# A fixed written issue order on TensorE and GpSimd, loads in pieces, and attention spread over the FFN halves

## The chip, the cores and the metric

The kernel runs on one core of one Trainium2 chip. The metric is the device time of that core in microseconds; a run's time is about 2 us longer than the span (first to last instruction) that its profile shows. Where a ratio stands, it is the mean time of one kernel's fast runs over that of the kernel before in the same rounds on the same chip, so it isn't quite the ratio of the medians that are quoted.

The engines are TensorE (PE in the profile, PEld its weight loads), VectorE (DVE), ScalarE (ACT), GpSimd (POOL) and SyncE (SP). "Issue" in the profile is time in which an engine waited for nothing that the profile shows.

## The reference

Four batches, eight heads, 768 positions, head size 64. Each head's sequence is cut into 8 blocks of 96. A small matrix P (8x8 for each batch and head) is normalized five times over rows and columns (Sinkhorn); it mixes the blocks of k and v; each block of q attends to its mixed block. The result goes through a gated feed-forward network (FFN).

```python
P = sort_net                                        # (4, 8, 8, 8)
for _ in range(5):
    P = np.exp(P - P.max(-1)); P = P / P.sum(-1); P = P / P.sum(-2)   # keepdims left out
k_sorted = einsum('bhij,bhjcd->bhicd', P, k_blocks)
v_sorted = einsum('bhij,bhjcd->bhicd', P, v_blocks)
x = softmax(q_blocks @ k_sorted.T / 8) @ v_sorted   # (3072, 512) after the reshape
g = x @ w_gate                                      # (512, 1536)
out = (silu(g) * (x @ w_val)) @ w_out               # (1536, 512)
```

## The kernel before

A tiling framework orders the instructions of each engine by priority and dependency; the program's text gives the priorities. TensorE does the block mixing with block-diagonal matrices made from P: the products `tkq` mix and transpose k and q together (q with an identity), `tv` mix v. For each unit (4 blocks of 2 heads) there are the scores `qk`, an exp on ScalarE, the attention-value product `av_ps`, on VectorE a reciprocal and the normalization `st`, and the transposition `x_ps` to the FFN's layout. One FFN half is 384 positions: 12 pairs of a gate product `g_ps` and a value product `v_ps` (4 matmuls each), and 3 output groups `o_ps` of 12 matmuls. There are 8 halves and 32 units.

```python
load_kq(0, [0, 24, 48, 72, 96]); make_identity(nc, ident)      # loads on GpSimd's queue
...
load_v(0, 2)
for it in range(5):                                             # Sinkhorn
    nc.scalar.activation(p_sb, p_sb, AF.Exp)
    nc.vector.reduce_sum(rowred[:, :, 0], p_sb, axis=AX.X); nc.vector.reciprocal(rowred, rowred)
    nc.vector.tensor_mul(p_sb, p_sb, rowred.to_broadcast([BH, NB, NB]))
    ...                                                         # the same for columns
# w_ps: P brought onto the partitions of k and v; rmix, vmix: the mixing matrices
...                                                             # weights, then batch 1 to 3
def emit_vch(pair):                                             # v's columns put side by side
    for s in range(4):
        eng = nc.gpsimd if pair else nc.vector
        eng.tensor_copy(vch[:, :, cs], nat[:, cs, :].transpose([0, 2, 1]))
...
emit_att(0)
for b in range(B):
    if b + 1 < B:
        emit_att(b + 1)
    emit_gv(b, 0); emit_gv(b, 1)
    emit_out(b, 0); emit_out(b, 1)
```

The softmax here doesn't subtract the row's maximum and nothing guards it: scores larger than these inputs give would overflow.

## Time and profile before

The median is 286.03 us (285.81 to 286.82). The profile below is of one execution of 287.63 us, with a mean granted clock of 0.968.

| stage (kernel before) | time, us | read from |
|---|---|---|
| normalization ends | 11.9 | timeline of VectorE |
| product w_ps starts | 13.6 | waits of TensorE |
| first score product / first attention-value product | 24.1 / 33.7 | timeline of TensorE |
| first gate product | 36.1 | timeline of TensorE |
| half clock | 35.6 to 49.3, 59.5 to 62.9 | clock records |
| last instruction | 285.9 | page |

The busy times and four rows of the page of the kernel before (each digit is the busy share of one fortieth of the span in tenths; PEclk is the granted TensorE clock):

```profile
PE 257.2 (90%) x2600; PEld 152.7 (53%) x2608; DVE 178.9 (63%) x383; ACT 121.7 (43%) x246; POOL 39.1 (14%) x51
PE   0077799969999999999999999999999999999993
PEclk9999955979999999999999999999999999999999
DMA  6999999999100122000000122000000220000021
```

TensorE is nearly always busy after the first tenth of the span. What there is to win lies at the start and in the two dips of the clock. The largest waits of TensorE before (in all, count, longest):

```profile
PE w_ps L148 <- DVE lmix L142: 13.6, 1, 13.6
PE tkq L193 <- issue: 2.5, 1, 2.5
```

The timeline of TensorE before (start, length, what, count, and in brackets the idle time ahead of it; the view ends at 61 us):

```profile
56.39 0.97 PE L193 MATMUL tkq<-rmix,kq 128*64 128x64 bf16 x45
59.90 1.33 PE L193 MATMUL tkq<-rmix,kq 128*64 128x64 bf16 x42 [2.54 <-issue]
```

### The profile page before, as it was taken

How to read it: one execution, taken by the hardware profiler on the slowest of the kernel's cores; microseconds unless marked ns; L12 is line 12 of the kernel's file. 1: busy time of each engine (PE TensorE's matmuls, PEld its weight loads, DVE VectorE, ACT ScalarE, POOL GpSimd, SP SyncE). 2: the span in 40 equal slices, each digit the busy share in tenths (PEclk: the TensorE clock that was granted, in tenths of full speed). 3: DMA queues.
4: the chain of work that ended last, by engine and by line, in shares of the span. 5: the costliest groups of instructions: out<-in, count | busy, mean ns of one | idle time of the engine just before them, and what ended most of it. 6: DMA issues, size and time to landing. Idle time of an engine off the chain costs nothing.

```text
span 285.9 us, 6221 instructions
## 1 busy us (share of the span) xinstructions
PE 257.2 (90%) x2600; PEld 152.7 (53%) x2608; DVE 178.9 (63%) x383; ACT 121.7 (43%) x246; POOL 39.1 (14%) x51
## 2 busy tenths in 40 slices
PE   0077799969999999999999999999999999999993
PEld 0066555746655446666655446666555445555441
DVE  6798746937988205789988304699885018888300
ACT  2036745437633215976534215764332134343211
POOL 8557421029500000000000000000000000000000
PEclk9999955979999999999999999999999999999999
DMA  6999999999100122000000122000000220000021
GB/s 99 198 203 197 200 213 204 220 214 214 38 0 1 39 110 76 2 2 0 3 0 2 38 110 76 2 2 2 0 0 2 111 102 10 0 0 3 37 110 73
DMA packets 13659, 20.84 MB, mean 73 GB/s; under 512 B 1088, under 2 KB 8768, under 8 KB 13632
## 3 DMA queue, kind: packets, MB, share of 16 engines
q0 software_dynamic: 10128, 14.16, 28.2%
q1 hardware_dynamic: 3504, 6.30, 5.8%
q8 instruction: 20, 0.33, 0.4%
q14 instruction: 7, 0.06, 0.1%
HBM read 28.32 MB, written 6.29 MB: 121 GB/s over the span
## 4 chain that ended last, share of the span: by engine, by line
PE 82%; DVE 11%; ACT 3%; issue 2%; ACTq 0%
PE v_ps L297 22%; PE g_ps L288 22%; PE o_ps L308 22%; PE av_ps L245 4%; PE qk L230 4%; PE tkq L193 3%; PE x_ps L255 3%; PE tv L214 3%; DVE kqt L180 2%; DVE vch L204 1%; DVE st L251 1%; ACT vt L182 1%; DVE vt L180 1%; ACT th_sb L291 1%; DVE colred L136 0%
## 5 line engine op out<-in xcount | busy, mean ns | idle before, releaser
L288 PE MATMUL g_ps<-xt,wg_sb 128*128 128x384 bf16 x384 | 84.8, 331 | 0.2 <-DVE h L299 0.2
L297 PE MATMUL v_ps<-xt,wv_sb 128*128 128x384 bf16 x384 | 82.1, 331 | 0.0
L291 ACT ACTIVATE th_sb<-g_ps 128x384 bf16<-128x384 f32 x96 | 47.1, 491 | 63.2 <-PE g_ps L288 62.6
L293 DVE SCALAR_TENSOR_TENSOR gs_sb<-th_sb,g_ps 128x384 bf16<-128x384 bf16 x96 | 52.9, 551 | 26.9 <-ACT th_sb L291 20.9
L308 PE MATMUL o_ps<-wo_sb,h 128*128 128x512 bf16 x280 | 62.4, 379 | 0.4
L299 DVE SCALAR_TENSOR_TENSOR h<-v_ps,gs_sb 128x384 bf16<-128x384 f32 x96 | 53.1, 553 | 9.0 <-PE v_ps L297 0.8
L297 PEld LDWEIGHTS <-wv_sb 128*128 128x128 bf16 x384 | 36.8, 98 | 24.5 <-issue 0.8
L288 PEld LDWEIGHTS <-wg_sb 128*128 128x128 bf16 x384 | 36.2, 99 | 23.5 <-issue 2.3
L308 PEld LDWEIGHTS <-h 128*128 128x128 bf16 x288 | 28.2, 98 | 33.6
L180 DVE CAST kqt<-tkq 128x512 bf16<-128x512 f32 x24 | 15.9, 688 | 33.9 <-PE tkq L193 33.9
L311 ACT COPY o_sb<-o_ps 128x512 f32<-128x512 f32 x24 | 14.1, 586 | 51.4 <-PE o_ps L308 51.4
L235 ACT ACTIVATE er<-qk 96x384 bf16<-96x384 f32 x64 | 27.1, 487 | 12.2 <-PE qk L230 12.2
L193 PE MATMUL tkq<-rmix,kq 128*64 128x64 bf16 x768 | 20.3, 212 | 5.5 <-issue 2.5
L193 PEld LDWEIGHTS <-kq 128*64 128x64 bf16 x768 | 17.7, 126 | 8.9 <-issue 7.9
L251 DVE TENSOR_TENSOR st<-av_ps,r_sb 96x512 bf16<-96x512 f32 x32 | 21.9, 684 | 0.8
L182 ACT CAST kqt<-tkq 128x512 bf16<-128x512 f32 x24 | 14.1, 586 | 15.7 <-PE tkq L193 15.6
L230 PE MATMUL qk<-kqt 64*128 64x96 bf16 x256 | 14.0, 217 | 1.9 <-DVE kqt L180 1.4
L245 PE MATMUL av_ps<-vt,er 96*128 96x65 bf16 x256 | 14.9, 202 | 0.2 <-ACT vt L182 0.2
L180 DVE CAST vt<-tv 96x512 bf16<-96x512 f32 x16 | 12.2, 785 | 2.7 <-PE tv L214 2.5
L182 ACT CAST vt<-tv 96x512 bf16<-96x512 f32 x16 | 12.5, 787 | 2.1 <-PE tv L214 1.8
L214 PE MATMUL tv<-vmix,vch 128*128 128x128 bf16 x128 | 12.4, 236 | 1.0 <-DVE vt L180 0.3
L255 PEld LDWEIGHTS <-st 96*128 96x128 bf16 x128 | 7.6, 101 | 10.5 <-DVE st L251 9.1
(43 smaller groups left out, 123.0 us busy)
## 6 DMA issues: line engine op xcount, KB each, us to landing
out_dram<-o_sb SPq DMA_DIRECT2D x24, 256.0 KB, 2.0
v<-in_v_dram POOLq DMA_DIRECT2D x8, 384.0 KB, 13.1
kq<-in_k_dram POOLq DMA_DIRECT2D x6, 384.0 KB, 11.6
kq<-in_q_dram POOLq DMA_DIRECT2D x6, 384.0 KB, 12.1
wg_sb<-in_moe_w_gate_dram POOLq DMA_DIRECT2D x6, 256.0 KB, 11.8
wv_sb<-in_moe_w_val_dram POOLq DMA_DIRECT2D x6, 256.0 KB, 11.1
wo_sb<-in_moe_w_out_dram POOLq DMA_DIRECT2D x1, 1536.0 KB, 18.9
kq<-in_k_dram POOLq DMA_DIRECT2D x4, 192.0 KB, 5.6
```

The costliest lines, as they stand in the source:

```text
L180: nc.vector.tensor_copy(dst, src)
L182: nc.scalar.copy(dst, src)
L193: nc.tensor.matmul(tp[two * D:(two + 1) * D, lc, :], lhsT=nat[:, cb * 8 + lc, :], rhs=rm[:, two, :], start=True, stop=True)
L230: nc.tensor.matmul(pss[two][:, i4, :], lhsT=flat[lo:lo + D, at:at + 128], rhs=kqt[lo:lo + D, 1, g, i, :], start=True, stop=True)
L235: nc.scalar.activation(e[:, 0:4 * C], pss[two][0:C].rearrange("p a c -> p (a c)"), AF.Exp, scale=scale)
L245: nc.tensor.matmul(av[:, two, i4, :], lhsT=es[two][:, i4 * C:i4 * C + 128], rhs=vt[:, 2 * g + two, half * 4 + i4, :], start=True, stop=True)
L288: nc.tensor.matmul(g_ps, lhsT=wg_sb[:, kc, ts(m, 128)], rhs=xt[:, kc, :], start=(kc == 0), stop=(kc == NKC - 1))
L291: nc.scalar.activation(th_sb, g_ps, AF.Tanh, scale=0.5)
L293: nc.vector.scalar_tensor_tensor(gs_sb, th_sb, 1.0, g_ps, op0=ALU.add, op1=ALU.mult)
L297: nc.tensor.matmul(v_ps, lhsT=wv_sb[:, kc, ts(m, 128)], rhs=xt[:, kc, :], start=(kc == 0), stop=(kc == NKC - 1))
L299: nc.vector.scalar_tensor_tensor(h_w[:, m, :], v_ps, 0.5, gs_sb, op0=ALU.mult, op1=ALU.mult)
L308: nc.tensor.matmul(o_ps, lhsT=h_w[:, m, ts(t3, 128)], rhs=wo_sb[:, m, :], start=(m == 0), stop=(m == NFC - 1))
```

## The change

The intent: TensorE and GpSimd issue in the order of the program text. Batch 0 and the weights are loaded in pieces, q is mixed while the normalization still runs, only batch 0's half of v is mixed at first, FFN half 0 starts after four units, and the attention of the next batch is spread between the products of the FFN halves. The core of the diff:

```diff
-    load_kq(0, [0, 24, 48, 72, 96])
+    man = tc.manual_schedule(engines={mybir.EngineType.PE, mybir.EngineType.Pool})
+    man.__enter__()
+    load_v(0, 0, HC)
     make_identity(nc, ident)
+    load_v(0, HC, C)
+    load_q(0, 0, HC); load_q(0, HC, C)
+    load_k(0, 0, HC); load_k(0, HC, C)
+    copy_v(nc.gpsimd, 0, lowr, 0)
+    load_gv(0, 256)
+    copy_v(nc.gpsimd, 0, lowr, 1)
+    load_gv(256, 512)
+    copy_v(nc.gpsimd, 0, lowr, 2)
+    copy_v(nc.scalar, 0, lowr, 3)
+    load_gv(512, 768)
     ...                                   # batch 1's k and q, the other weights, v of batch 1
+    for cb in range(6):
+        half_chunk(0, 1, cb, "s", tags[cb % 2])           # q of batch 0, before w_ps
     ...                                   # w_ps, rmix, vmix as before, through a copy w_sb
+    for cb in range(6):
+        half_chunk(0, 0, cb, "vs"[cb % 2], tags[cb % 2])  # k of batch 0
+    ...                                   # qk(0, 0..3) between 8 v_chunk; then av and xtr of 4 units
+    def merge(main, side):                # side items placed in proportion to main's time
     ...
-    emit_att(0)
-    for b in range(B):
-        if b + 1 < B:
-            emit_att(b + 1)
-        emit_gv(b, 0); emit_gv(b, 1); emit_out(b, 0); emit_out(b, 1)
+    merge(ffn(0), units(0, range(4, 8)))
+    nc_b1 = attention(1)
+    merge(ffn(1), nc_b1)
+    for b in range(1, B):
+        first, second = split(attention(b + 1)) if b + 1 < B else ([], [])
+        merge(ffn(2 * b), first)          # ffn(n): 12 pairs of n, 3 output groups of n - 1
+        merge(ffn(2 * b + 1), second)
+    for t3 in range(3):
+        outp(2 * B - 1, t3)
```

A half chunk mixes k or q alone, with 32 matmuls of half the height, where a whole chunk mixes both: 384 matmuls in place of 192 for batch 0.

## The prediction

> **What bounds the kernel now.** TensorE: 257 of 286 us busy on the page, without gaps from 63 to 281 us in the timeline. By start-to-start times four gate or value matmuls cost 0.65 us and twelve output matmuls 2.6 us, so one FFN half is 15.7 + 7.8 = 23.5 us and eight are 188 us at full clock. Where attention units are packed between FFN pairs (126 to 140 us) their period is 2.17 us, VectorE's own work in it (0.55 + 0.55 + 0.20 + 0.68 + half of 0.35). The waste lies before 63 us: TensorE starts at 13.6 us, the first FFN matmul comes at 36.1 us, the clock records show 0.5 from 35.6 to 49.3 us and from 59.5 to 63.0 us, and there are 2.5 us of idle at 57.4 us, where batch 1's last k/q piece had not landed (the queue runs at 200 GB/s until 71 us). [...] the records change in multiples of 3.41 us, and at 28.8 us the tv matmuls go from 107 to 55 ns.
>
> **What the change does, from the issue order on each engine.**
> 1. Batch 0's V evictions (0.79 us each) before the first AV are halved, exps overlap them, and q is mixed during Sinkhorn. But v, q and k land in that order (2.36 MB, about 16.7 us at the rate of before), and four AV units run bare: AV, reciprocal 0.20, transpose copy 0.35, normalise 0.68, about 1.7 us each. I estimate the first FFN matmul at 36 us (34 to 38): no earlier than now.
> 2. From there FFN half 0 is dense, not 3 FFN matmuls per 2.5 us at half clock. Full clock returns after about 5 us: 4 us gained.
> 3. Batch 1's k/q is queued before the later weights (there at about 31 us, needed near 55 us): the 2.5 us idle and its 1.7 us of half clock go.
> 4. Units are spread over two FFN halves for batches 2 and 3: at most 0.2 us gained on each of 20 units, 3 to 4 us.
> 5. Costs: batch 1's V mixing is a second pass, 64 more matmuls, about 2.3 us. Batch 1's attention is pressed into one FFN half: four qk in a row wait for exps on ScalarE (about 2 us), and its last three units run bare after the last output group (about 3 us, perhaps 1.7 us of half clock near 85 to 90 us). Batches 2 and 3 end with one bare unit, 1 us each.
>
> **Sum.** 36 + 188 (FFN) + 39 (attention left) + 2.5 (cold clock) + 10 (stalls) + 4.5 (last copy and store) = about 280 us.
>
> Predicted 280.5 us, range 272 to 289. Faster by over 2%: 0.48; within 2%: 0.46; slower: 0.06.
>
> **What the profile would show.** First gate matmul at 34 to 38 us; half clock for 3 to 7 us from there, then 1.0; no wait for batch 1's k/q; a stretch of low TensorE share near 85 to 90 us with transposes waiting for the normalise step; the last three output groups unchanged.
>
> **What would make it wrong.** A faster start (half-height k/q chunks under 0.6 us would bring the FFN to 33 us); clock drops of several windows after the bare units; Pool's transposing copies (2.9 us each) in its in-order queue holding up loads; ScalarE, which takes all k/q and v evictions, delaying the tanh and so the gate matmuls.

The terms come to 280.0 us. But the 5 us after which full clock was to return, and with them the 4 us gained and the 2.5 us of cold clock, are the author's estimate. In the trace before, half clock lasted 13.7 us from 35.6 us and 3.4 us from 59.5 us; what the change made of it stands under the result.

## The result

The changed kernel takes 303.48 us (303.03 to 303.96, four runs), against 286.09 us (285.81 to 286.82) for the kernel before in the same rounds: ratio 1.0604 (95% interval 1.0577 to 1.0630). It is slower by 6%. The same rows of the page, after:

```profile
PE 260.3 (86%) x2864; PEld 154.5 (51%) x2864; DVE 163.4 (54%) x357; ACT 132.3 (44%) x263; POOL 52.1 (17%) x51
PE   0057667999998959999999989999999999999994
PEclk9999999999999996999999999999999999999998
DMA  6999999198084000100100000000000001000011
```

TensorE is busy for a smaller share of the span than before (86% against 90%), above all in slices 3 to 7. The clock row needs care: ahead of the first clock record, at 54.1 us, it shows full clock, but in this run four gate matmuls take 1.28 us up to 54.1 us and 0.65 us later, so TensorE was at half clock until then. Behind the first gate product there are 12.5 us of half clock in all (48.4 to 54.1 and 112.2 to 119.0 us), against 16.6 us before (36.1 to 49.3 and 59.5 to 62.9), a window behind the last product left out in both, so the clock isn't where the time went. In two parts:

| | before | predicted | after |
|---|---|---|---|
| first gate product, us | 36.1 | 36 | 48.4 |
| from there to the end of the span, us | 249.8 | 244.5 | 253.7 |

The predicted 280.5 us is a run's time, about 2 us longer than a span, so the second row missed by 9 us as it stands and by about 11 in like terms.

**The start, 12.3 us late.** The largest waits of TensorE after:

```profile
PE tkq L200 <- DVE rmix L163: 18.7, 1, 18.7
PE av_ps L279 <- DVE st L285: 5.7, 6, 1.0
PE x_ps L296 <- DVE st L285: 3.8, 4, 1.0
PE tkq L200 <- issue: 3.4, 2, 2.3
PE qk L259 <- ACT e_all L266: 1.8, 3, 0.7
```

The first mixing product waits for a VectorE copy into rmix until 18.7 us, though q's first piece landed at 11.5 us. The timeline of VectorE after shows what held that copy up:

```profile
6.64 2.27 DVE L173 TENSOR_TENSOR p_sb<-p_sb,rowred 32x64 f32<-32x64 f32 x1
8.95 0.25 DVE L174 TENSOR_REDUCE colred<-p_sb 32x8 f32<-32x64 f32 x1
9.46 5.16 DVE L176 TENSOR_TENSOR p_sb<-p_sb,colred 32x64 f32<-32x64 f32 x1
15.41 1.93 DVE L173 TENSOR_TENSOR p_sb<-p_sb,rowred 32x64 f32<-32x64 f32 x1
17.89 0.21 DVE L176 TENSOR_TENSOR p_sb<-p_sb,colred 32x64 f32<-32x64 f32 x1
18.51 0.44 DVE L163 COPY rmix<-ident 64x64 bf16<-64x64 bf16 x4
20.46 0.68 DVE L340 TENSOR_TENSOR lmix<-p_sb,selk 32x512 bf16<-32x512 f32 x1
```

The same multiplication takes 0.21 us when it is left alone, and here once 2.27, once 5.16 and once 1.93 us, while reductions and reciprocals between them keep their length. The timeline of GpSimd after, in the same time:

```profile
6.10 2.73 POOL L113 COPY vch<-v 64x1536 bf16<-64x1536 bf16 x1 [1.08 <-DMA v<-in_v_dram]
10.31 2.77 POOL L113 COPY vch<-v 64x1536 bf16<-64x1536 bf16 x1
14.46 2.79 POOL L113 COPY vch<-v 64x1536 bf16<-64x1536 bf16 x1
```

Each long multiplication ends within 0.2 us of the end or the start of one of these new GpSimd copies. The multiplications read p_sb and rowred or colred, both in SBUF (the memory that this program keeps its tiles in, apart from the products of TensorE, which go to PSUM). The reductions at 6.18 and 14.95 us, which read one tile, keep their 0.21 us beside the copies. The multiplication that began at 9.46 us did so while GpSimd by its records only issued loads (8.79 to 10.33 us), and stood through a whole copy (10.31 to 13.08) and two more issues, until 14.62 us. The issues alone don't lengthen a multiplication: those at 17.89, 19.45 and 20.22 us kept 0.21 us beside them. No run shows why the one at 9.46 us stood. The normalization ends at 20.4 us in place of 11.9, and w_ps starts at 24.0 in place of 13.6.

Then k is mixed. The timeline of TensorE after:

```profile
23.98 0.59 PE L346 MATMUL w_ps<-selb,lmix 32*64 32x4 bf16 x16
25.18 0.59 PE L200 MATMUL tkq<-rmix,kq 64*64 64x32 bf16 x15 [0.61 <-DVE rmix L355]
26.88 3.60 PE L200 MATMUL tkq<-rmix,kq 64*64 64x32 bf16 x128 [1.10 <-issue]
32.80 1.51 PE L200 MATMUL tkq<-rmix,kq 64*64 64x32 bf16 x49 [2.33 <-issue]
34.99 0.50 PE L259 MATMUL qk<-kqt 64*128 64x96 bf16 x8 [0.68 <-ACT kqt L182]
```

All of k landed by 17.2 us, and yet there are two stalls that wait for nothing shown. Between them lie exactly 128 matmuls, with their weight loads 256 instructions. The DMA records have 16 KB reads of TensorE's instructions starting at 24.5, 30.5, 36.6 and 42.7 us: one for every 3.6 us of this work, but 6.1 us apart. TensorE stands for 1.10 us ahead of the 128 matmuls and for 2.33 us behind them. That it waits there for these reads is the reading so far; the runs with held loads below test it.

Behind the k mixing come scores and v mixing, for which the prediction gives no size of its own, and the four bare attention-value units (bare: with no FFN product between them). These take 7.5 us up to the first gate product, where four times 1.7 us was estimated; the second, third and fourth each begin with 1.02 to 1.04 us of waiting for VectorE to empty the one result buffer.

**From the first gate product on, 9 us more than predicted.** TensorE's gaps of over 0.15 us behind it come to 9.2 us, against 3.8 before. Three of the waits lie close together at the end of half 1. The timeline of TensorE after, and then the same kernel in windows of 3.40 us (the clock records of both kernels between the first and the last product change in steps of 3.41 us; columns: window, its length, busy us and count of PE, PEld, DVE, ACT, POOL, then the granted clock, DMA share, GB/s):

```profile
109.61 0.43 PE L279 MATMUL av_ps<-vt,e_all 96*128 96x65 bf16 x8 [1.04 <-DVE st L285]
111.26 0.43 PE L279 MATMUL av_ps<-vt,e_all 96*128 96x65 bf16 x8 [1.05 <-DVE st L285]
112.90 0.50 PE L296 MATMUL x_ps<-ident,st 96*128 96x96 bf16 x4 [1.04 <-DVE st L285]
```

```profile
108.80:112.20 3.40, 1.20 (x24) 0.91 (x24) 2.35 (x8) 0.00 (x0) 0.00 (x0) 0.99 0.20 77
112.20:115.60 3.40, 2.70 (x12) 1.35 (x12) 1.36 (x4) 0.49 (x1) 0.00 (x0) 0.50 0.00 0
```

The window with 1.20 us of work in 3.40 was followed by half clock, for two windows (112.2 to 119.0 us). In the kernel before, windows with 1.96 us (from 32.2 us) and 1.26 us (from 56.1 us) were, and in e12_coarse below one with 1.71 us.

Where the time from the first gate product to the end goes, by product, for four kernels (from the start of a group's first matmul to the start of the next group's first, summed; so a wait counts to the group ahead of it; the last two kernels are experiments below; a few before-kernel units had begun ahead of its first gate product and some of its groups mix in the order, so single rows are good to about 1 us):

| product | before | after | e12_coarse | e8_best |
|---|---|---|---|---|
| gate and value | 134.4 | 136.8 | 134.4 | 133.4 |
| output | 67.0 | 67.6 | 67.2 | 69.3 |
| k and q mixing | 16.8 | 12.8 | 12.8 | 13.5 |
| v mixing | 4.8 | 6.6 | 6.6 | 6.3 |
| scores | 9.6 | 10.9 | 9.8 | 7.3 |
| attention-value | 9.0 | 7.5 | 9.0 | 8.0 |
| transposition | 8.2 | 11.5 | 10.1 | 4.8 |
| sum | 249.8 | 253.7 | 249.8 | 242.6 |

### The profile page after: what moved, and what is told of

It is laid out like the page before. It is cut to its first block, busy times and chain, and to the rows that moved or that the text cites. A ratio compares the mean times of both kernels' runs of the same rounds, so it can differ in the third digit from the quotient of the medians.

```text
span 302.1 us, 6710 instructions
## 1 busy us (share of the span) xinstructions
PE 260.3 (86%) x2864; PEld 154.5 (51%) x2864; DVE 163.4 (54%) x357; ACT 132.3 (44%) x263; POOL 52.1 (17%) x51
## 4 chain that ended last, share of the span: by engine, by line
PE 82%; DVE 10%; ACT 4%; issue 2%; DMA 1%; ACTq 0%
PE g_ps L309 22%; PE o_ps L328 21%; PE v_ps L318 21%; PE tkq L213 4%; PE tkq L200 4%; PE av_ps L279 3%; PE qk L259 3%; DVE st L285 2%; DVE p_sb L176 2%; PE x_ps L296 2%; PE tv L234 2%; DVE p_sb L173 2%; ACT o_sb L331 1%; ACT vt L182 1%; DVE xt L180 1%
## 5 line engine op out<-in xcount | busy, mean ns | idle before, releaser
L182 ACT CAST kqt<-tkq 128x512 bf16<-128x512 f32 x45 | 25.0, 589 | 21.3 <-PE tkq L213 12.3
L113 POOL COPY vch<-v 64x1536 bf16<-64x1536 bf16 (+1 forms) x11 | 30.5, 2810 | 18.8 <-DMA v<-in_v_dram 13.2
L266 ACT ACTIVATE e_all<-qk 96x384 bf16<-96x384 f32 x64 | 27.7, 483 | 11.1 <-PE qk L259 11.1
L200 PE MATMUL tkq<-rmix,kq 64*64 64x32 bf16 x384 | 11.0, 211 | 22.8 <-DVE rmix L163 18.7
L200 PEld LDWEIGHTS <-kq 64*64 64x64 bf16 x384 | 10.7, 152 | 22.9 <-DMA kq<-in_q_dram 11.6
L279 PE MATMUL av_ps<-vt,e_all 96*128 96x65 bf16 x256 | 14.3, 200 | 6.5 <-DVE st L285 5.7
L283 DVE RECIPROCAL r_sb<-av_ps 96x8 f32<-96x8 f32 x32 | 6.4, 199 | 24.4 <-PE av_ps L279 24.4
L182 ACT CAST vt<-tv 96x512 bf16<-96x512 f32 x26 | 17.7, 752 | 2.5 <-PE tv L244 1.2
L279 PEld LDWEIGHTS <-e_all 96*128 96x128 bf16 x256 | 11.9, 102 | 11.3 <-DVE st L285 7.4
L213 PEld LDWEIGHTS <-kq 128*64 128x64 bf16 x576 | 11.3, 113 | 9.4 <-issue 9.4
## 6 DMA issues: line engine op xcount, KB each, us to landing
wg_sb<-in_moe_w_gate_dram POOLq DMA_DIRECT2D x6, 256.0 KB, 11.4
```

The source lines that it names most:

```text
L113: eng.tensor_copy(dst, src)
L182: nc.scalar.copy(dst, src)
L200: nc.tensor.matmul(tp[two * D:(two + 1) * D, lc, :], lhsT=nat[rows, cb * 16 + lc, :], rhs=rmix[b][rows, two, a].rearrange("p g i -> p (g i)"),
L266: nc.scalar.activation(e[:, 0:4 * C], pss[two][0:C].rearrange("p a c -> p (a c)"), AF.Exp, scale=scale)
L279: nc.tensor.matmul(o[:, two, i4, :], lhsT=e[:, i4 * C:i4 * C + 128], rhs=vt[:, 2 * g + two, half * 4 + i4, :], start=True, stop=True)
```

## The experiments

Theories that the experiments tell apart:

- A: GpSimd's early copies block VectorE and so the normalization, in the multiplications (A1) and in the rmix copies (A2); the first gate product is late for that.
- R: in phases of very short products, TensorE waits for its own instructions (1.10 and 2.33 us after), because their refills come late while data loads fill the DMA.
- W: with one result buffer, and with units bunched behind each other, the attention units wait for VectorE and ScalarE, and the gaps bring back the half clock (112.2 to 119.0 us after).
- Rivals: the start is held by loads, or by refills of a fixed duration; VectorE's own rate sets the units' period; spreading costs as much at each switch as it saves.

### Sums kept in PSUM (e1_psum)

```diff
-    rowred = const.tile([BH, NB, 1], FP32)
-    colred = const.tile([BH, 1, NB], FP32)
+    red_ps = psum.tile([BH, 2, NB], FP32, name="red_ps", tag="av", bufs=1)
+    rowred = red_ps[:, 0, :].unsqueeze(2)
+    colred = red_ps[:, 1, :].unsqueeze(1)
```

> The changed kernel with the two Sinkhorn scale vectors in PSUM, so that VectorE's Sinkhorn multiplications read only one operand from SBUF; Pool's copies and loads stay. Theory A [...]: the multiplications take 0.2 to 0.3 us again where they took 1.9 to 5.2, the last Sinkhorn step ends near 12.5 us and not 20.4, the first gate matmul comes at about 41 us and not 48.4, total about 296 us (295 to 298). Rival B ([...] anything else of Pool that slows VectorE whatever it reads): multiplications stay at 2 us or more, total 303.

Measured 298.94 us (ratio 1.042, interval 1.036 to 1.048), just outside the 295 to 298 expected. The timeline of VectorE in this run:

```profile
6.78 0.21 DVE L174 TENSOR_TENSOR p_sb<-p_sb,red_ps 32x64 f32<-32x64 f32 x1
8.91 8.45 DVE L163 COPY rmix<-ident 64x64 bf16<-64x64 bf16 x4
17.39 0.21 DVE L174 TENSOR_TENSOR p_sb<-p_sb,red_ps 32x64 f32<-32x64 f32 x1
```

Every multiplication takes 0.21 us now: the second SBUF operand was what blocked them (A1). But the four rmix copies that now come up in GpSimd's time take 8.45 us in place of 0.44, and the multiplication behind them waits in order. The repair of one instruction moved the block to the next. w_ps starts at 20.9 us and the first gate product at 43.7 us; 4.5 us of the 7.5 us expected came.

### One identity copy on GpSimd (e2_ident), and both repairs (e3_both)

```diff
+    nc.gpsimd.tensor_copy(rmix0[R:2 * R, :, 1, :, :], idq)   # ahead of GpSimd's first v copy
     copy_v(nc.gpsimd, 0, lowr, 0)
     ...
-    for b in range(B):                                       # VectorE's copies: batch 0's is gone
+    for b in range(1, B):
```

> The changed kernel with batch 0's identity block of the mixing matrix written by Pool before its first copy, not by VectorE behind the fourth Sinkhorn iteration; Sinkhorn is left as slow as it is. Theory A: q mixing starts at about 11.6 us (when q has landed) but the weights matmul still waits for Sinkhorn at about 21.2 us, so only the 2.8 us between 21.2 and 24.0 are gained: about 300.5 us. Rival C (what costs the start is the identity copy's place in VectorE's order, not the blocked multiplications): the start moves by about 7 us and the total is about 296.

> Both edits together. Theory A: as with the PSUM edit alone within 1 us (about 296), because with Sinkhorn fast the identity copies come at about 10 us and are no longer late; the start is then bound by the landing of q and k and by two waits of TensorE for instruction blocks (1.1 and 2.3 us in the changed kernel). Rival C: another 3 us or more below the PSUM edit alone.

Measured 298.99 us for the first (ratio 1.0438), between theory A's 300.5 and rival C's 296. q's mixing starts at 11.4 us, the multiplications are blocked as before (2.04, 5.16 and 1.93 us), w_ps starts at 21.0, where A had it, and the first gate product comes at 43.6 us: 3.0 us come from the earlier w_ps, and most of the rest from the k mixing, where one stall of 1.9 us is left of the two (3.4 us).

Measured 295.62 us for both (ratio 1.0317, interval 1.027 to 1.037). That is 3.3 us below the PSUM edit alone, which is what rival C expected of the pair, so by the totals the place of the identity copy in VectorE's order counts too. The profile can't show how: its execution, with a span of 297.0 us, was 3 us longer than the timed ones (293.0 to 294.0). In it the three rmix copies left on VectorE take 8.26 us and the first gate product stays at 43.7 us. As long as the early GpSimd copies are there, these profiles show one VectorE instruction or the other blocked.

### No early copies on GpSimd (e5_nopool)

```diff
-    copy_v(nc.gpsimd, 0, lowr, 0)          # and 1, 2; and 3 on ScalarE
     ...
+    for s in range(4):                     # after rmix and vmix; the first line only makes it wait
+        nc.vector.tensor_copy(vch3[lowr, 0, 24 * s:24 * s + 1], w_sb[0:R, 0, s:s + 1])
+        copy_v(nc.vector, 0, lowr, s)
```

> Only batch 0's four early transposing copies move from GpSimd and ScalarE to VectorE, made to wait for the mixing matrices. Theory A (GpSimd's early copies block VectorE, whatever VectorE does with two SBUF operands or as an SBUF copy): the normalization ends near 12 us instead of 20.4, the weights product w_ps starts near 13, every VectorE multiplication in it takes 0.2 to 0.3 us and every identity copy under 0.5, the first gate product comes near 40 us instead of 48.4, and the total falls to about 293 (291 to 295). Rival B (the start is held by loads and instruction refills, and the blocking only hides behind them): the first gate product stays at 43 or later, as in the run with both partial repairs, and the total stays at 295.5 or more.

Measured 296.45 us (ratio 1.0363, interval 1.033 to 1.040). The timeline of VectorE, then of TensorE:

```profile
6.54 0.21 DVE L169 TENSOR_TENSOR p_sb<-p_sb,rowred 32x64 f32<-32x64 f32 x1
9.69 0.44 DVE L159 COPY rmix<-ident 64x64 bf16<-64x64 bf16 x4
11.64 0.68 DVE L336 TENSOR_TENSOR lmix<-p_sb,selk 32x512 bf16<-32x512 f32 x1
```

```profile
16.70 0.59 PE L342 MATMUL w_ps<-selb,lmix 32*64 32x4 bf16 x16
25.93 1.51 PE L196 MATMUL tkq<-rmix,kq 64*64 64x32 bf16 x49 [2.88 <-issue]
```

k's evictions (the copies of its products out of PSUM), which alternated between VectorE and ScalarE, went to ScalarE alone in the same edit. No VectorE instruction of the normalization is stretched, and it ends at 11.6 us, 8.8 us earlier: A holds. The first gate product comes at 41.4 us, 7.0 us earlier. Two expectations were missed. w_ps was expected near 13 us and starts at 16.7, although lmix is ready at 12.3: in the written order it stands behind q's 192 matmuls, which the fixed order can't pass. And the total was expected at 291 to 295; at 296.45 it lies where rival B had it (295.5 or more), though the first gate product doesn't. That product came 1.4 us later than expected, and from there to the end the kernel took 253.0 us, hardly less than the changed kernel (253.7), with the same two windows of half clock behind the bare units.

### Loads held while k is mixed (e6_hold, e11_hold, e10_both)

```diff
-    load_gv(256, 512)                      # and all later loads, from GpSimd's early order
     ...
     for cb in range(6):
         half_chunk(0, 0, cb, ...)
+    held = const.tile([1, 1], BF16)        # GpSimd waits here for the last k chunk
+    nc.gpsimd.tensor_copy(held, kqt_tile(0)[0:1, GI * C - 1:GI * C])
+    load_gv(256, 512)                      # and all later loads
```

The first two are the changed kernel with this alone (the second is the first once more, timed); the third has it together with the edit of e5_nopool.

> The changed kernel, with all loads after the first weight pieces held back until k is mixed, so that the data queue is empty during the k mixing. Theory R (the two stalls of 1.1 and 2.3 us in the k mixing are refills of TensorE's instructions [...]): both shrink below 0.4 us, and the k mixing takes about 6 us instead of 9. Rival S (a refill takes that long whatever the data queue does, or the stalls have another cause): stalls of 1 us and more stay in the k mixing. The total isn't to be read from this run, since the weights come late on purpose: it may be 300 to 315.

> The changed kernel with only the loads held, timed this time (the look had one execution, 296.9). If holding the loads is worth the refill stalls and the 3 us of half clock less that the look showed, it is 297 (295.5 to 298.5); if that one execution was a chance, 301 or more.

> The run without early GpSimd copies, and in the same kernel the loads after the first weight pieces held until k is mixed. If blocked VectorE and refills behind loads are two separate losses, the stall of 2.9 us in the k mixing goes too and what the two save at the start adds up: the first gate product comes at about 37 to 38 us (41.4 without the hold), and the total is about 292 (290 to 294). Rival (the two overlap, or held weights come late): the first gate product stays after 40 us, or gate products wait for weights, and the total is 295 or more.

The look took 296.91 us (one execution), the timed run 299.20 us (ratio 1.0443, interval 1.039 to 1.049), slower than the 295.5 to 298.5 expected. The timeline of TensorE in the timed run, then of the third kernel:

```profile
24.73 5.30 PE L189 MATMUL tkq<-rmix,kq 64*64 64x32 bf16 x192 [0.62 <-DVE rmix L344]
30.71 0.50 PE L248 MATMUL qk<-kqt 64*128 64x96 bf16 x8 [0.68 <-ACT kqt L171]
```

```profile
17.92 4.96 PE L185 MATMUL tkq<-rmix,kq 64*64 64x32 bf16 x177 [0.91 <-issue]
```

The 192 matmuls of k run through in 5.30 us without a stall. Nothing on TensorE was changed: R holds, as far as the loads are what makes the refills late. (The hold took GpSimd's issuing of the loads out of this stretch as well as their traffic; no run tells the two apart.) A single read of 16 KB takes no longer beside loads: in the changed kernel the four reads from 24.5 to 42.7 us took 0.94 to 1.09 us each, and its later ones, of which most have no loads beside them, 0.88 to 1.45. With loads those four reads are 6.1 us apart. Without loads they follow 3.5 us apart in the third kernel (15.5, 19.0 and 22.5 us) and 5.1 and 3.9 us apart in the timed run, and keep up with the work. What makes the next read start late isn't seen in the records and stays open. Where some of the first weights still load, 0.91 us of the stall is left.

The first gate product comes at 44.0 us with the hold alone, and at 37.3 us with both edits (total 293.08 us, ratio 1.0230, interval 1.017 to 1.029, as expected): 4.4 us from the hold and 7.0 us from the copies make 11.4, and both together bring 11.1, so they are two separate losses. But the hold isn't the refills alone. In the changed kernel the k mixing shrinks from 9.1 to 5.3 us; in the third it shrinks from 9.5 to 6.5 us, and another 1.5 us come from q, whose first piece lands at 9.7 in place of 11.4 us. That the sums agree so well is partly chance, and in these executions the loads hold the start a little. The timed run was slower than the look, 299.2 against 296.9: its profiled execution has 6.8 us of half clock in two pieces, the look's 3.4 us. Such single windows came and went between executions of one kernel: of the four runs of e9_av2 below, three show a mean clock of 0.992 or 0.993, and the one at 1.0 took 2 us less.

With 37.3 us the start is nearly that of the kernel before (36.1), yet the kernel is still 2.3% slower than it. So there is a second part to explain, behind the first gate product.

### The last units earlier (e4_tail)

```diff
-    def merge(main, side):
-        total_m = sum(c for c, _ in main)
+    def merge(main, side, lead=0.0):       # side items end ahead of main's last 3.9 us
+        total_m = sum(c for c, _ in main) - lead
     ...
-    merge(ffn(0), units(0, range(4, 8)))
-    merge(ffn(1), nc_b1)
+    merge(ffn(0), units(0, range(4, 8)) + nc_b1[:12])      # batch 1's k and q mixing too
+    merge(ffn(1), nc_b1[12:], lead=3.9)
```

> The changed kernel with the start left alone: batch 1's k/q mixing moves into FFN half 0, and the attention units of each batch end before the last output group of their FFN half, so that no AV unit runs bare. If the bare units and the half clock after them (112 to 119 us) cost what the trace shows (three waits of 1.04 us and about 3 us of half clock in FFN half 1, one wait of 1.04 us each in halves 3 and 5), the total falls by 6 to 8 us, to about 296.5. If the units only move their waits elsewhere (VectorE sets their pace), it falls by less than 3.

Measured 299.32 us (ratio 1.0455, interval 1.039 to 1.052): 4 us gained, between the 6 to 8 expected and the 3 of the rival. The profile is of an execution with a span of 300.2 us, longer than the timed ones (296.7 to 298.8); in it the part from the first gate product to the end takes 251.1 us in place of 253.7, and one window of half clock is left. Three of the four timed runs show a mean clock of 1.0. The bare units at the ends are gone, but other waits stay where two items of the same kind follow each other: two transpositions behind the last attention-value product (1.31 us), two pairs of score products (0.74 us for ScalarE's exp).

### Two result buffers (e9_av2)

```diff
-        av_ps = psum.tile([128, 2, 512], FP32, name="av_ps", tag="av", bufs=1)
         for two in range(2):
+            av_ps = psum.tile([128, 4, D + 1], FP32, name="av_ps", tag="av", bufs=2)
             ...                                    # one reciprocal and one st for each head
```

> Only the attention-value result is split into one tile per head with two buffers[...]. Theory W (with one buffer each attention-value product waits about 1 us for VectorE to empty it): the four bare units before the first gate product take about 4.5 us instead of 7.2, the waits for st fall below 0.5 us each, and the total falls by 4 to 6 us, to about 298. Rival X (VectorE's own rate sets the period, so a second buffer buys nothing, and twice as many VectorE instructions cost as much as they save): the bare units still take 6.5 us or more and the total stays within 1.5 us of 303.5.

Measured 300.02 us (ratio 1.0477, interval 1.042 to 1.053): 3.5 us gained, less than the 4 to 6 that theory W expected, more than rival X's 1.5. The waits of TensorE:

```profile
PE x_ps L295 <- DVE st L284: 3.5, 5, 0.9
PE av_ps L279 <- DVE st L284: 2.9, 7, 0.7
```

The wait of attention-value products halved from 5.7 us to 2.9. Up to the first gate product the four bare units take 6.1 us in place of 7.5 (the expectation left out the last transposition, and wanted 4.5 in place of 7.2): VectorE now fills their time, with two reciprocals (0.18 us), two st (0.41) and the copy of x (0.36) for each unit. Both theories were partly right: the buffer was one limit, VectorE's rate is the next.

### Whole chunks, k and q ahead of v (e7_full)

On top of e5_nopool:

```diff
-    load_v(0, 0, HC) ...; load_q ...; load_k ...
+    load_k(0, 0, HC) ...; load_q ...; load_v ...
-    for cb in range(6):
-        half_chunk(0, 1, cb, "s", tags[cb % 2])
     ...                                    # w_ps first, then
-    for cb in range(6):
-        half_chunk(0, 0, cb, "s", tags[cb % 2])
+    for cb in range(12):
+        kq_chunk(0, cb, "s" if cb < 9 else "vs"[cb % 2], tags[cb % 2])
```

> The run without early GpSimd copies, and besides k and q load ahead of v and batch 0 is mixed in whole chunks of k and q together, so half as many TensorE instructions. Theory A with R (start held by the blocked normalization, and then by instruction refills in a phase of very short products): w_ps near 13 us, mixing 14 to 23, first gate product at 35 to 38, total about 289 (287 to 292). Rival: if the loads hold the start, the first gate product comes no earlier than in the run with copies on VectorE alone (about 40) and the total is 292 or more.

Measured 289.86 us (ratio 1.0140, interval 1.011 to 1.017), as expected. w_ps starts at 12.4 us, and the first gate product comes at 35.0 us, earlier than in the kernel before. Batch 0 is mixed in 192 matmuls instead of 384, in one run without a stall, though no load is held:

```profile
13.54 5.34 PE L209 MATMUL tkq<-rmix,kq 128*64 128x64 bf16 x192 [0.53 <-DVE rmix L348]
```

The run changes the order of the loads, the place of w_ps and the size of the chunks at once; how much each brings isn't shown. The kernel is still 1.4% slower: from the first gate product on it takes 252.8 us against 249.8.

### One unit to a slot (e8_best), and the same without it (e12_coarse)

On top of e7_full: two result buffers, two score units placed among the four bare units, whose x copies go to ScalarE, batch 0's matrices made ahead of the other batches', and spreading by count instead of by estimated time:

```diff
-            todo.append((1.3, lambda m=m: gv(n, m)))
-            if n > 0 and m % 4 == 3:
-                todo.append((2.6, lambda m=m: outp(n - 1, m // 4)))
+            todo.append(lambda m=m: gate(n, m))            # 4 matmuls
+            todo.append(lambda m=m: val(n, m))             # 4 matmuls
+            if n > 0 and m % 4 == 3:
+                for part in range(4):                      # 3 of the 12 matmuls each
+                    todo.append(lambda m=m, part=part: outp(n - 1, m // 4, part))
     ...
-            while k < len(side) and done_s + side[k][0] <= total_s * done_m / total_m + 1e-9:
+            while k < len(side) and k + 1 <= len(side) * (i + 1 - skip) / (len(main) - lead - skip) + 1e-9:
     ...
-    merge(ffn(0), units(0, range(4, 8)))
-    merge(ffn(1), nc_b1)
+    merge(ffn(0), units(0, range(4, 8))[2:] + tkqs + rest[:2], lead=0)
+    merge(ffn(1), tvs + rest[2:], lead=3, skip=3)
```

e12_coarse is e8_best with this last diff taken back (the two score units stay among the bare ones). The diff holds three things: units one to a slot, batch 1's k and q mixing in half 0, and an end of the units ahead of the half's end.

> The run with whole chunks, and besides: batch 0's mixing matrices before the copies and the other batches' after, one attention-value tile per head with two buffers, two score units among the bare attention-value units, and the attention units of the other halves spread one to a slot between single gate, value and output pieces, ending before the half does. If the found causes are the whole story (blocked VectorE, order of the first products, one buffer, bunched units and the half clock after them): the first gate product at about 31 us, no idle gap over 0.7 us from there to the last output group, no half clock after the first warm one past 45 us, 246 us from the first gate product to the end, total about 279 (276 to 283), so faster than the kernel before by some 2.5 per cent. Rival (spreading itself costs: each switch between short and long products adds a lead-in that is not regained): from the first gate product to the end 250 us or more, total 283 or more.

> The best kernel (279.3) without its fine spreading: everything else is kept, and the units are merged with the output products as in the changed kernel, in clumps behind whole gate-value pairs and whole output groups, batch 1 wholly in half 1. If spreading is what wins the steady part, the first gate product stays at about 34, from there to the end it takes 249 to 251 us instead of 242.6, and the total is 285 to 288. Rival (the two attention-value buffers and the better start win it all): from the first gate product to the end 245 or less, total 281 or less.

e8_best: 279.30 us (279.11 to 280.00), ratio 0.9760 (interval 0.972 to 0.980). It beats the kernel before by 2.4% and the changed kernel by 8%. e12_coarse: 286.43 us, ratio 1.0005 (interval 0.997 to 1.005). Waits of TensorE in e12_coarse, then in e8_best:

```profile
PE x_ps L291 <- DVE st L280: 3.8, 5, 0.9
PE av_ps L275 <- DVE st L280: 2.0, 5, 0.7
PE qk L255 <- ACT e_all L262: 1.8, 3, 0.7
```

```profile
PE x_ps L291 <- DVE st L280: 1.6, 4, 0.7
PE av_ps L275 <- DVE st L280: 0.7, 1, 0.7
```

The clock row of the page of e8_best shows the dip at the start and none after:

```profile
PEclk9995579999999999999999999999999999999999
```

Both have their first gate product at 34.4 us. From there e12_coarse takes 249.8 us and e8_best 242.6. The table above says where the 7.2 us are: 5.3 less in transpositions and 2.5 in scores, with the waits behind them mostly gone, 1.0 each in attention-value products and in gate and value products (one window of half clock less); the output groups, now cut in pieces, take 2.1 more. So the diff as a whole wins 7 us and its rival is refuted. No run has the single slots alone: e4_tail had the other two things in the changed kernel and gained 4 us, so part of the 7 may be theirs. e8_best's total was met, but its two halves weren't. The first gate product was expected at 31 us and came at 34.4; the trace has a wait of 1.75 us of the first tv product for VectorE's copies of v, and half clock from 21.3 to 38.4 us, and how much each costs isn't shown. Behind it 246 us were expected, and 242.6 were measured.

## Why the prediction was wrong

1. **"I estimate the first FFN matmul at 36 us (34 to 38)": 48.4 us.** This is the step that failed first, and in it the overlap "q is mixed during Sinkhorn": q's first piece had landed at 11.5 us, but its mixing began at 18.7, behind a copy on a VectorE that GpSimd's copies blocked. The estimate rested on landing times and on lengths of single instructions, with nothing that lengthens VectorE's early work or interrupts TensorE's mixing. Taking the early GpSimd copies away brings 7.0 us (e5_nopool) and holding the loads another 4.1 (e10_both): 11.1 of the 12.3 us. The four bare units with one buffer took 7.5 us where four times 1.7 was estimated, which is 0.7 us more. The copies are named in the last paragraph of the prediction, but as a danger to loads, not to VectorE.
2. **"From there FFN half 0 is dense ... 4 us gained."** It is dense, and full clock returned after 5.7 us, where about 5 had been the estimate. The half clock behind the first gate product fell from 16.6 us before to 12.5 us; but more waits (9.2 us behind the first gate product, against 3.8) took the gain back.
3. **"the 2.5 us idle and its 1.7 us of half clock go", because "batch 1's last k/q piece had not landed".** The reading was wrong: that piece had landed 13 us before, and an instruction read starts at 57.49 us within the idle time. That the stall of the kernel before is a late refill too is argued from this alone; no run changed the kernel before. In the changed kernel this wait is gone, as forecast, but the reason given for it was wrong: that was luck.
4. **"Units are spread over two FFN halves ... 3 to 4 us."** It didn't come in the changed kernel: its units stand in clumps behind whole pairs and groups (x waits 3.8 us, scores 1.8 us). Spread one to a slot, with batch 1's mixing moved and an earlier end, they brought 7.2 us (e8_best against e12_coarse). That spreading can win was right; what it takes was missed.
5. **The costs** were named rightly in kind: bare last units, then half clock ("perhaps 1.7 us" near 85 to 90 us expected; 6.8 us at half clock, so about 3.4 us lost, found at 112 to 119; the late start explains 12 us of the shift), scores waiting for exps (1.8 us against 2), the second v pass.
6. **"39 (attention left) + 2.5 (cold clock)"** are the terms of the sum that were mis-sized behind the first gate product; "10 (stalls)" was about right. The 253.7 us hold 188 for the FFN and 4.5 for the tail as predicted, about 6 us lost to the 12.5 us at half clock (2.5 predicted), and 9.2 us of gaps, which leaves about 46 for attention (39 predicted). Part of these 7 us lies in the switches: a group of four gate or value matmuls takes 0.74 us up to a score product (54.76 to 55.50 us) or a k and q mixing product (71.57 to 72.31 us), and 0.65 to 0.66 up to the next gate or value group or an attention-value product (58.12 to 58.77 us). The rest is open.

"Slower by over 2%" had been given 0.06: the sum had no term for one engine slowing another, nor for TensorE waiting for its instructions.

## What to carry to other kernels

- Before moving a helper copy to GpSimd, look at what VectorE does in the same microseconds: here a multiplication with two operands in SBUF took up to 5.16 us in place of 0.21, through several of GpSimd's instructions, and with that repaired the block passed to four plain SBUF copies, 8.45 us in place of 0.44 (e1_psum).
- In the fixed order an instruction that wasn't ready, or wasn't needed yet, held what stood behind it (w_ps had its operand at 12.3 us and started at 16.7, behind q's products, in e5_nopool), so write the product that others wait for first; in a phase of very short matmuls, use fewer and larger ones (192 in 5.34 us without a stall in e7_full), or keep bulk loads out of it (192 in 5.30 us in e11_hold, against 9.1 us in the changed kernel).
- Spreading short units between long products paid (7.2 us, e8_best against e12_coarse) when each had a long product on both sides and the last ended early enough (both were changed together here, with one thing more); in clumps part of the waits only moved (e4_tail: 4 us gained where 6 to 8 were expected).
